# A dense layer with SiLU: the first slab of w1 loaded in two halves, on two queues

## The chip, the core and the metric

The kernel runs on one core of a Trainium2 chip. A core has TensorE (matrix products; its weight loads are listed as PEld), VectorE, ScalarE, GpSimd and SyncE, each with its own list of instructions; SyncE and ScalarE also issue the DMA transfers of this kernel. The metric is the device time of one execution in microseconds (us). Lower is better.

## The reference

```python
h = jnp.einsum("bsd,df->bsf", x, w1)     # x 1 x 2048 x 640, w1 640 x 1728, bfloat16
h = jax.nn.silu(h)
out = jnp.einsum("bsf,fd->bsd", h, w2)   # w2 1728 x 640
```

Two matrix products, with SiLU between them; input, weights and result are bfloat16.

## The kernel before

The 2048 rows of x are cut into four chunks of 512. The first product is computed transposed: for a tile of 128 columns of w1 (ft, 13 full tiles and one of 64) and a chunk, the 640 values of the sum are taken in five steps of 128 (k, `DT` = 5). One matmul has a 128 x 128 block of w1 as its weights and a 128 x 512 block of x, transposed, as its moving operand. x arrives transposed by transposing DMAs (`turned`, line 120), one for each chunk and k. w1 goes to `w1s`, w2 to `w2s`, and the last 64 columns and rows are handled apart.

For the first chunk the order is chosen so that work can begin with little data. The first eight tiles (`FA` = 8) are computed k by k (`k_pass`, line 178): pass k takes x's block k and slab k of w1, which is 128 rows of w1 by 1024 columns, 256 KB, and adds into the eight PSUM banks. Before each pass TensorE waits for the transpose `ld_x[k]` and the slab `ld_k[k]` (line 186). After pass 4 the remaining tiles 8 to 12 follow (line 197), from two larger transfers, tiles 8 to 10 and tiles 11 to the end (`FG`, line 117). Then come the other chunks, the 64-column tail, and the second product, whose results are copied out by VectorE and ScalarE and stored by SyncE.

The order of the DMA issues on SyncE is written out by hand: transpose 0, transpose 1, slab 1, transpose 2, slab 2, and so on to slab 4, then the two larger w1 transfers, then the transposes of the other chunks and w2. Slab 0 alone is issued by ScalarE (line 132).

A program begins with a barrier that the framework puts in: each engine drains and reports, GpSimd waits for all reports and lets all go, and each engine waits for that. The kernel moves instructions about it. `ahead_of_start` (line 98) puts an instruction ahead of an engine's drain: the zeroing of `z`, transpose 0 and slab 0. `barrier_wait_here` (line 109) moves an engine's own wait to a later place: for SyncE behind the w1 transfers (line 141), for TensorE behind the dummies (line 167). Dummies (line 161) are matmuls on the zeros in `z`, 256 columns each, whose result nobody reads; twelve of them keep TensorE busy until the first data is there. ScalarE runs one SiLU on a small buffer (line 145), so that its table is loaded early.

Of the kernel before, what the change touches and what calls it, by code (L numbers as in the profile page):

```python
# [9 lines left out]
def bass_standalone__dense_activation_silu__prompt_kernel(  # L10
# [13 lines left out]
    P = 128  # L24
    NB = 8
    BANK = 512
    DT = D // P
# [10 lines left out]
    pe, act, dve, pool, sp = nc.tensor, nc.scalar, nc.vector, nc.gpsimd, nc.sync  # L38

    with ExitStack() as es:  # L40
        def sb(name, shape, dtype):
            return es.enter_context(nc.sbuf_tensor(name, shape, dtype))

        xT = sb("xT", [P, DT, S], bf16)
        w1s = sb("w1s", [P, DT, F], bf16)
# [13 lines left out]
        def sem(name):  # L59
            s = es.enter_context(nc.semaphore(name))  # L60
            count[s.name if hasattr(s, "name") else name] = 0
            return [s, 0]

        def tick(ins, s, n=1):
            ins.then_inc(s[0], n)
            s[1] += n
            return (s, s[1])

        def wait(eng, *points):
            for pt in points:  # L70
                if pt is None:
                    continue
                s, v = pt
                key = (id(eng), id(s))
                if seen.get(key, 0) < v:
                    eng.wait_ge(s[0], v)
                    seen[key] = v
# [6 lines left out]
        def load(eng, out_ap, in_ap):  # L84
            s = sem(f"s_ld{n_dma[0]}")
            n_dma[0] += 1
            return tick(eng.dma_start(out=out_ap, in_=in_ap), s, 16)  # L87

        ET = mybir.EngineType

        def preamble(engine, opcode):
            lst = nc.main_func.blocks[0].instructions
            return next(
                i for i, ins in enumerate(lst)
                if ins.opcode == opcode and ins.engine == engine
            )

        def ahead_of_start(emit, engine):
            lst = nc.main_func.blocks[0].instructions
            n = len(lst)  # L100
            r = emit()
            lst = nc.main_func.blocks[0].instructions
            new = lst[n:]
            del lst[n:]
            at = preamble(engine, "Drain")
            lst[at:at] = new
            return r

        def barrier_wait_here(engine):
            lst = nc.main_func.blocks[0].instructions  # L110
            lst.append(lst.pop(preamble(engine, "EventSemaphore")))

        w1_v = w1.rearrange("(dt p) f -> p dt f", p=P)
        w2_v = w2[0:F0, :].rearrange("(ft p) d -> p ft d", p=P)

        FA = 8
        FG = [(8, 11), (11, FT)]

        def turned(c, dt, s):
            return tick(sp.dma_start_transpose(  # L120
                out=xT[:, dt, c * SCH:(c + 1) * SCH],
                in_=xf[c * SCH:(c + 1) * SCH, dt * P:(dt + 1) * P],
            ), s, 16)

        def load_k(eng, k):
            return load(eng, w1s[:, k, 0:FA * P], w1_v[:, k, 0:FA * P])

        ld_w1 = {}
        s_x = [sem(f"s_x{k}") for k in range(DT)]
        p_z = ahead_of_start(lambda: tick(dve.memset(z[:, :], 0.0), s_dve), ET.DVE)  # L130
        ld_x = [ahead_of_start(lambda: turned(0, 0, s_x[0]), ET.SP)]
        ld_k = [ahead_of_start(lambda: load_k(act, 0), ET.Activation)]
        for k in range(1, DT):
            ld_x.append(turned(0, k, s_x[k]))
            ld_k.append(load_k(sp, k))
        for a, b in FG:
# [24 lines left out]
        def dummies(n):  # L161
            for _ in range(n):
                pe.matmul(ps[:, 3, 0:HB], lhsT=z[:, 0:P], rhs=z[:, :], start=True, stop=True)  # L163

        wait(pe, p_z)
        dummies(12)
        barrier_wait_here(ET.PE)

        def mm(o, l, r, start, stop, shared=False):
            return pe.matmul(o, lhsT=l, rhs=r, start=start, stop=stop, skip_group_check=shared)  # L170

        def silu(out_ap, in_ap, bank, after):
            wait(act, after)
            r = tick(act.activation(out=out_ap, in_=in_ap, func=ACT.Silu), s_act)  # L174
            bank_free[bank] = r
            return r

        def k_pass(k):
            for ft in range(FA):
                ins = mm(ps[:, ft, :], w1s[:, k, ft * P:(ft + 1) * P], xT[:, k, 0:SCH],  # L180
                         start=(k == 0), stop=(k == DT - 1), shared=True)
                if k == DT - 1:
                    silu(hT[:, ft, 0:SCH], ps[:, ft, :], ft, tick(ins, s_pe))

        for k in range(DT):
            wait(pe, ld_x[k], ld_k[k])
            k_pass(k)

        nxt = [FA]

# [169 lines left out]
```

## Time and profile before

| | us |
|---|---|
| median of five executions | 126.42 |
| the five, lowest to highest | 125.83, 125.83, 126.42, 127.14, 127.69 |
| the profiled execution, its own time | 125.92 |
| span of the profiled execution | 124.6 |
| TensorE busy with matmuls | 121.4 (97%) |
| TensorE busy with weight loads | 55.0 (44%) |
| ScalarE busy | 38.2 (31%) |
| VectorE busy | 7.5 (6%) |
| transpose 0, from issue to landing | 3.3 |
| slab 0 (ScalarE), from issue to landing | 2.6 |
| slabs 1 to 4 (SyncE), from issue to landing | 3.1, 3.2, 3.3, 3.4 |

The span runs from the first to the last instruction of one execution; the rest of that execution's time lies around it. All times inside the span count from its start. Line numbers such as L170 are those of the kernel before; L170 is the helper through which all real matmuls go, L163 the dummies, L120 the transposing loads, L87 all other DMA transfers, L345 the framework's own instructions. A name such as SPq is an engine's instruction queue, here SyncE's, and the time beside it is what the issue takes, not the transfer. The landing of a transfer is when its completion is seen.

### The profile page before, as it was taken

The numbers are of one execution on the slowest core, as the hardware profiler recorded it, in microseconds if no ns is written. First come the engines' busy times: TensorE is split into PE (matmuls) and PEld (weight loads), VectorE is DVE, ScalarE is ACT, GpSimd is POOL, SyncE is SP. The second block draws the span as 40 slices with busy tenths as digits, with TensorE's granted clock in tenths as the row PEclk, the third lists the DMA queues.
The fourth block names the chain that finished last, engine by engine and source line by source line (L and its number), as shares of the span: only waits on it lengthen the run. The fifth ranks groups of instructions, "written<-read, shape, count | busy, mean of one in ns | idle before, by whom it ended". The sixth has DMA issues, their size and how long they took to land.

```text
span 124.6 us, 1336 instructions
## 1 busy us (share of the span) xinstructions
PE 121.4 (97%) x575; PEld 55.0 (44%) x586; DVE 7.5 (6%) x12; ACT 38.2 (31%) x66; POOL 0.3 (0%) x5
## 2 busy tenths in 40 slices
PE   8999999999999999999999999999999999999993
PEld 5343444444444444444434444444434444444452
DVE  0000000000000000000002020200012220102021
ACT  3000985555555555555530101010012101010100
POOL 1000000000000000000000000000000000000000
PEclk9999999999999999999999999999999999999999
DMA  5899959444795000000000000000002468111112
GB/s 129 178 231 240 249 114 81 107 104 90 188 388 196 0 5 0 3 0 0 0 0 0 5 0 0 0 0 0 0 0 67 65 216 299 53 53 53 53 59 99
DMA packets 19398, 10.35 MB, mean 83 GB/s; under 512 B 13505, under 2 KB 18753, under 8 KB 19393
## 3 DMA queue, kind: packets, MB, share of 16 engines
q1 hardware_dynamic: 19248, 10.02, 31.6%
q10 hardware_dynamic: 144, 0.26, 0.7%
q8 instruction: 4, 0.07, 0.2%
q14 instruction: 2, 0.01, 0.0%
HBM read 4.51 MB, written 2.62 MB: 57 GB/s over the span
## 4 chain that ended last, share of the span: by engine, by line
PE 87%; SPq 7%; DMA 4%; issue 1%; ACT 0%
PE ps L170 87%; SPq L120 5%; DMA w1s<-in_w_dram 4%; SPq L87 2%; SPq L345 0%; ACT o_sb L232 0%
## 5 line engine op out<-in xcount | busy, mean ns | idle before, releaser
L170 PE MATMUL ps<-xT,w1s 128*128 128x512 bf16 (+1 forms) x275 | 60.0, 385 | 0.5 <-DMA xT<-in_x_dram 0.2
L170 PE MATMUL ps<-w2s,hT 128*128 128x512 bf16 (+2 forms) x216 | 45.2, 366 | 0.3
L170 PEld LDWEIGHTS ps<-xT,w1s 128*128 128x128 bf16 (+1 forms) x280 | 26.5, 100 | 34.1 <-issue 2.8
L174 ACT ACTIVATE hT<-ps 128x512 bf16<-128x512 f32 x52 | 30.1, 606 | 28.6 <-PE ps L170 28.6
L170 PEld LDWEIGHTS ps<-w2s,hT 128*128 128x128 bf16 x221 | 20.9, 98 | 24.4 <-issue 1.1
L232 ACT CAST o_sb<-ps 128x512 bf16<-128x512 f32 (+1 forms) x8 | 4.4, 546 | 42.2 <-PE ps L170 37.2
L230 DVE CAST o_sb<-ps 128x512 bf16<-128x512 f32 (+1 forms) x9 | 6.1, 677 | 101.1 <-PE ps L170 101.1
L170 PE MATMUL ps<-hT,w2s 128*128 128x512 bf16 x51 | 11.3, 379 | 0.1
L170 PEld LDWEIGHTS ps<-hT,w2s 128*128 128x128 bf16 x52 | 5.1, 98 | 6.1
L232 ACT CAST oT<-ps 128x512 bf16<-128x512 f32 x2 | 1.1, 588 | 11.0 <-PE ps L170 11.0
L163 PE MATMUL ps<-z 128*128 128x256 bf16 x12 | 2.7, 419 | 0.4 <-DVE z L130 0.4
L170 PE MATMUL ps<-w2t,hTt 64*128 64x512 bf16 (+2 forms) x17 | 2.2, 366 | 0.0
L230 DVE CAST oT<-ps 128x512 bf16<-128x512 f32 x2 | 1.3, 686 | 13.7 <-PE ps L170 13.7
L163 PEld LDWEIGHTS ps<-z 128*128 128x128 bf16 x12 | 1.6, 144 | 1.0 <-DVE z L130 0.4
L145 ACT ACT_TABLE_LOAD x1 | 1.3, 1283 | 1.9 <-PEq L345 1.9
L174 ACT ACTIVATE hTt<-ps 128x512 bf16<-128x512 f32 x2 | 1.2, 597 | 1.1 <-PE ps L170 1.1
L170 PEld LDWEIGHTS ps<-w2t,hTt 64*128 64x128 bf16 x17 | 0.7, 94 | 1.4 <-issue 0.8
L170 PE MATMUL ps<-hTt,w2t 64*128 64x512 bf16 x4 | 0.6, 381 | 0.0
L170 PEld LDWEIGHTS ps<-hTt,w2t 64*128 64x128 bf16 x4 | 0.1, 94 | 0.4 <-issue 0.4
L145 ACT ACTIVATE warm<-warm 128x32 f32<-128x32 f32 x1 | 0.2, 229 | 0.0
L130 DVE MEMSET z<- 128x128 uint32 x1 | 0.2, 165 | 0.2 <-issue 0.2
L143 POOL MEMSET warm<- 128x32 f32 x1 | 0.1, 124 | 1.5 <-POOLq L345 1.5
(4 smaller groups left out, 0.4 us busy)
## 6 DMA issues: line engine op xcount, KB each, us to landing
out_dram<-o_sb SPq DMA_DIRECT2D x15, 160.0 KB, 1.9
w2s<-in_w_dram SPq DMA_DIRECT2D x1, 1120.0 KB, 5.9
w1s<-in_w_dram SPq DMA_DIRECT2D x4, 256.0 KB, 3.3
w2s<-in_w_dram SPq DMA_DIRECT2D x1, 960.0 KB, 8.1
w1s<-in_w_dram SPq DMA_DIRECT2D x1, 480.0 KB, 4.8
w1s<-in_w_dram SPq DMA_DIRECT2D x1, 400.0 KB, 5.6
xT<-in_x_dram SPq DMA_TRANSPOSE x20, 2.9
w1s<-in_w_dram ACTq DMA_DIRECT2D x1, 256.0 KB, 2.6
```

The lines of the kernel that those rows point to most:

```text
L87: return tick(eng.dma_start(out=out_ap, in_=in_ap), s, 16)
L120: return tick(sp.dma_start_transpose(out=xT[:, dt, c * SCH:(c + 1) * SCH], in_=xf[c * SCH:(c + 1) * SCH, dt * P:(dt + 1) * P],), s, 16)
L130: p_z = ahead_of_start(lambda: tick(dve.memset(z[:, :], 0.0), s_dve), ET.DVE)
L143: p_warm = tick(pool.memset(warm[:, :], 0.0), s_pool)
L145: act.activation(out=warm[:, :], in_=warm[:, :], func=ACT.Silu)
L163: pe.matmul(ps[:, 3, 0:HB], lhsT=z[:, 0:P], rhs=z[:, :], start=True, stop=True)
L170: return pe.matmul(o, lhsT=l, rhs=r, start=start, stop=stop, skip_group_check=shared)
L174: r = tick(act.activation(out=out_ap, in_=in_ap, func=ACT.Silu), s_act)
L230: r = tick(dve.tensor_copy(out=out_ap, in_=in_ap), s_dve)
L232: r = tick(act.copy(out=out_ap, in_=in_ap), s_act)
```

## The change

Slab 0 is cut into two halves of four tiles. ScalarE issues the first half ahead of its drain, SyncE the second half behind transpose 0. Transpose 1 and slab 1 are also put ahead of SyncE's drain. TensorE waits before pass 0 for the first half only, and for the second half between tiles 3 and 4 of pass 0. There are 15 dummies instead of 12, and TensorE's barrier wait moves from behind the dummies to behind pass 0.

```diff
-        ld_k = [ahead_of_start(lambda: load_k(act, 0), ET.Activation)]
-        for k in range(1, DT):
+        FH = FA // 2
+        ld_k0a = ahead_of_start(
+            lambda: load(act, w1s[:, 0, 0:FH * P], w1_v[:, 0, 0:FH * P]), ET.Activation)
+        ld_k = [ahead_of_start(
+            lambda: load(sp, w1s[:, 0, FH * P:FA * P], w1_v[:, 0, FH * P:FA * P]), ET.SP)]
+        ld_x.append(ahead_of_start(lambda: turned(0, 1, s_x[1]), ET.SP))
+        ld_k.append(ahead_of_start(lambda: load_k(sp, 1), ET.SP))
+        for k in range(2, DT):
             ld_x.append(turned(0, k, s_x[k]))
             ld_k.append(load_k(sp, k))
...
         wait(pe, p_z)
-        dummies(12)
-        barrier_wait_here(ET.PE)
+        dummies(15)
...
             for ft in range(FA):
+                if k == 0 and ft == FH:
+                    wait(pe, ld_k[0])
...
         for k in range(DT):
-            wait(pe, ld_x[k], ld_k[k])
+            wait(pe, ld_x[k], ld_k[k] if k else ld_k0a)
             k_pass(k)
+            if k == 0:
+                barrier_wait_here(ET.PE)
```

## Prediction, made before the changed kernel was run

> **What bounds the kernel now.** I read the chain of waits first, because the page gives TensorE 97% busy and a change at the start can only pay if something at the start holds the end.
>
> ```profile
> 1.25 0.05 issue
> 1.30 0.37 SPq L345
> 1.67 0.07 issue
> 1.74 1.14 SPq L120
> 2.88 0.05 issue
> 2.94 0.57 SPq L87
> 3.51 0.06 issue
> 3.57 1.12 SPq L120
> ...
> 8.27 0.04 issue
> 8.31 0.58 SPq L87
> 8.89 0.04 issue
> 8.93 4.79 DMA w1s<-in_w_dram
> 13.72 0.05 issue
> 13.77 10.32 PE ps L170 x47
> ```
>
> Columns: start, length, what. Up to 8.93 us the end hangs on SyncE writing out DMA issues one after another, then on one transfer (w1 columns of tiles 8 to 10), which lands at 13.72. From there it is TensorE without a hole to the end. So each us added to SyncE's list before 8.93 is added to the end, if the transfer keeps its 4.79 us; TensorE work before 13.7 counts only if it becomes later than that landing.
>
> How much later could it be? The timeline of the start shows TensorE's rate:
>
> ```profile
> 0.39 2.74 PE L163 MATMUL ps<-z 128*128 128x256 bf16 x12 [0.39 <-DVE z L130]
> ...
> 3.34 0.13 PEld L170 LDWEIGHTS ps<-xT,w1s 128*128 128x128 bf16 x2 [0.69 <-DMA xT<-in_x_dram]
> ...
> 3.75 0.15 PEld L170 LDWEIGHTS ps<-xT,w1s 128*128 128x128 bf16 x1 [0.28 <-issue]
> 4.17 0.15 PEld L170 LDWEIGHTS ps<-xT,w1s 128*128 128x128 bf16 x1 [0.27 <-issue]
> ```
>
> Weight loads, one per tile, start 0.427 us apart up to 6.31 us. The windows of the later passes hold eight tiles in 1.72 to 1.73 us (6.53 to 8.25, 8.25 to 9.98), 0.216 each. So the whole pass k=0, eight tiles, ran at half rate (3.34 to about 6.5), and full rate began near 6.31, although the granted clock reads 1.00 in every window. Pass 3 then began at 10.00 instead of 9.98 and pass 4 at 11.81 instead of 11.72, both on w1; the tiles after pass 4 could have begun at 13.54 but waited to 13.77. Without these three waits (0.02 + 0.09 + 0.23) TensorE would have been there at 13.43: its cover is 0.34 us.
>
> **The change part by part.** The sum is made against the profiled execution: span 124.6 us, its own time 125.92, so 1.32 lies around the span. The median of the runs shown is 126.42, 0.50 above it.
>
> *Half of slab 0 from ScalarE to SyncE.* ScalarE's one issue (0.38 us at 0.12) stays one issue. SyncE gets one more, between transposes 0 and 1. All four w1 issues that follow a transpose take 0.57 to 0.58 us, the two that follow another load 0.43 and 0.53; the new one follows a transpose, and ScalarE's whole slab also has one row per partition, so half the bytes need not shorten it: 0.575 + 0.05 for the step between = 0.625 us on SyncE.
>
> *Transpose 1 and slab 1 ahead of SyncE's drain.* They were behind it; the order of the DMAs among themselves stays, only the drain moves.
>
> ```profile
> L345 ACTq DRAIN  x1: 145/145/145, 0.5 to 0.5; - x1
> L345 SPq DRAIN  x1: 367/367/367, 1.3 to 1.3; - x1
> ```
>
> SyncE's drain behind a transpose took 0.367, ScalarE's behind a plain load 0.145. The new place is behind a plain load. New list of SyncE: transpose 0 to 1.25; half slab 1.30 to 1.87; transpose 1 from 1.92 (was 1.74); slab 1 from 3.10 (was 2.94); drain from 3.72; transpose 2 from 3.94 with the short drain, 4.16 with the long one (was 3.57). Everything behind, tiles 8 to 10 too, is late by 0.37 to 0.59. I take 0.37, since what stands before an issue visibly matters (0.58 against 0.43 above).
>
> Does that reach the landing? Two readings. The Trainium skill, page "DMA: Bandwidth & Descriptors", section "Issuing engines are not separate DMA queues", says that all issuers share the same 16 DMA engines and that spreading issues saves only the sequencer's time, "which is usually small relative to the DMA itself". By that the same bytes arrive at the same time and the sum is 0: 125.92. The row says otherwise: slabs 1 to 4, issued every 1.79 us, land 3.1, 3.2, 3.3 and 3.4 us after issue, nearly constant, so there the issue sets the pace and the DMA engines follow. Only the 0.3 us of growth, and 4.79 for the last transfer, show some backlog, which could swallow a part of the delay. By the row the sum is +0.37. Bounds: 0 (all swallowed) and +0.59.
>
> *The first transpose beside half the traffic.* It landed 3.30 us after issue, the second 2.8, with fewer bytes beside it: at best 0.5 us earlier. Worth nothing here, because of the next part.
>
> *Three more dummies.* Twelve started 0.213 us apart from 0.39; fifteen occupy TensorE to about 3.57. The first real matmul moves from 3.34 to 3.57: +0.23, on TensorE alone. The work until full rate is then 0.23/0.427 = 0.53 tile less, made up at 0.216 each: +0.115 us later at tile 8, 13.55 against the 13.43 above. Cover: the landing at 13.72 + 0.37 = 14.09. Cost nothing; without that cover, 0.12.
>
> When does full rate begin? The page "TensorE: Matmul & The Clock Gate", Part 1, gives half clock by default and full clock after a busy window of about 3.4 us that runs freely, not from the kernel's start. By the row, 6.31, the forecast stands. By the rule with dummies counted from 0.39 it may begin anywhere from 3.8 to 7.2. At 3.8 TensorE gains (6.31 - 3.8)/2 = 1.25 us and loses it all in waits for w1; at 7.2 it loses 0.45, still inside the new cover of 14.09 - 13.55 = 0.54. The trace has one phase only.
>
> *A wait in the middle of pass 0* for the second half of slab 0. Behind it on TensorE are tiles 4 to 7 and all later work. It is needed at 3.57 + 4 x 0.427 = 5.27. Issued at 1.30, it lands between 3.9 (ScalarE's slab, 2.6 us) and 4.7 (the slowest slab, 3.4). I take 4.4, by slab 1's 3.1. Cost nothing; the cover is 0.6 to 1.4 us. Transpose 1 and slab 1 shift by 0.16 to 0.18, so slab 1 lands at 6.2, needed at 6.6.
>
> *Barrier.* SyncE's drain now ends at 3.9 to 4.1 instead of 1.67, so the other engines are let go 2.2 to 2.4 us later: ScalarE's table load from 1.89 to about 4.2, done with its warm-up by 5.8; its first real activation is at 12.2. VectorE and GpSimd have nothing due. TensorE's own wait now stands behind pass 0, which ends after 5.3 at any clock: free. Cover 6 us and more than 1 us.
>
> Sum: +0.37 on the landing, the rest hidden: 125.92 + 0.37 = 126.29 for an execution like the profiled one, 126.42 + 0.37 = 126.8 for a median like the one shown.
>
> **Rivals.** *Swallowed:* the DMA backlog takes the delay in, and the landing stays near 13.72. For it: growing landing times, 4.79 for the last one. Against it: the even pace before. TensorE's 13.55 is still covered: 125.9 by the profile, 126.4 by the median.
>
> *Fewer late starts of the full clock:* the five runs spread by 1.86 us, more than a DMA floor explains; if in some of them TensorE reached full rate late because of the idle 0.2 us between dummies and transpose, the unbroken dummies would bring all to the floor. The floor itself is up by 0.37, so 126.3 in the median; to be over 1% faster (under 125.16) it would have to beat the shortest run, 125.83, by 0.7, for which I find no mechanism.
>
> *Slower: full rate comes one window later.* If zeros, or the later start of real work, put it off by 3.41 us to 9.7, then 14.4 tiles run at 0.427 and 25.6 at 0.216 from 3.57 on: tile 8 at 15.24, against 13.77: +1.47, 127.4 by the profile and 127.9 by the median. It decides from about 7.4 us on, where TensorE passes the landing at 14.09. For it: the spread of the runs before, which such phases would give. Against it: 12 dummies with a hole sufficed at 6.31, and 15 without a hole give no less activity.
>
> *It does not do what it says:* splitting the slab was to start pass 0 sooner; with dummies to 3.57 it starts later whatever lands. That is inside the forecast.
>
> **How the numbers follow.** The landing moves by 0.2 to 0.6: chance 0.50, 126.8. Swallowed 0.17, 126.4. Fewer late starts 0.11, 126.3. A later full clock 0.22, 127.9. The range leaves out the tails: 125.9 (swallowed, with a median half a us low, as the spread allows) to 127.9. A change under 1%, 1.26 us, is what a measurement of this kernel can hardly tell from none, with runs from 125.83 to 127.69. Of the first three cases 0.06 may fall below 125.16 for reasons I do not see; the later clock gives 0.21 over 127.68.
>
> **What would show it.** In the changed kernel's profile: transpose 2 issued at 3.9 to 4.2; the tiles 8 to 10 transfer issued at 9.3 to 9.5 and landing at 14.1 to 14.3, again the last wait before an unbroken TensorE; first real matmul at 3.57; no wait in pass 0. The forecast is wrong if w1 lands no later than 13.8, if the spacing stays 0.427 beyond 7.4 us, or if TensorE halts in the middle of pass 0.

## The result and the profile after

| | kernel before | changed kernel |
|---|---|---|
| median of all executions | 126.49 us (79) | 126.28 us (44) |
| lowest to highest | 125.28 to 127.69 | 125.72 to 127.14 |
| lowest tenth below, highest tenth above | 125.54, 127.46 | 125.81, 126.60 |
| profiled execution, its span | 125.92, 124.6 | 126.19, 124.9 |

The ratio is 1.0004, 95% interval 0.9988 to 1.0019: no change. This ratio leaves out executions more than 1.5% above the fastest of the same kernel, which here takes 14 of 79 from the kernel before and none from the changed one; the medians and tenths above count all. They show what one number hides: the lowest tenth rose by 0.27 us, the highest fell by 0.86.

The chain of waits of the changed kernel, start, length, what (from here on, line numbers are those of the run that is shown; in the changed kernel L169 is the dummies, L175 the helper of the real matmuls, L354 the framework):

```profile
1.25 0.06 issue
1.31 0.56 SPq L87
1.87 0.06 issue
1.93 1.14 SPq L120
3.07 0.04 issue
3.12 0.58 SPq L87
3.69 0.06 issue
3.75 0.13 SPq L354
3.88 0.07 issue
3.94 1.13 SPq L120
...
8.70 3.50 DMA w1s<-in_w_dram
12.19 0.14 issue
12.33 0.59 PE ps L175 x2
```

SyncE's list stands as forecast: the new half-slab issue at 1.31, the drain (L354) at 0.13, transpose 2 at 3.94 for 3.57. But the last wait is now slab 4, issued at 8.70, landing at 12.19 (11.68 before). The transfer of tiles 8 to 10, the last wait before, landed at 13.64 (13.72 before) although it was issued 0.39 later: it took 4.3 us for 4.8. Slab 4 held pass 4 until 12.33, and tile 8 began eight tiles later, at 14.05, against 13.77: +0.28.

The timeline of the start:

```profile
0.39 3.38 PE L169 MATMUL ps<-z 128*128 128x256 bf16 x15 [0.39 <-DVE z L130]
...
3.57 5.61 PE L175 MATMUL ps<-xT,w1s 128*128 128x512 bf16 x20
...
4.42 0.15 PEld L175 LDWEIGHTS ps<-xT,w1s 128*128 128x128 bf16 x1 [0.28 <-issue]
4.85 0.78 PEld L175 LDWEIGHTS ps<-xT,w1s 128*128 128x128 bf16 x4 [0.28 <-issue]
```

Real work begins at 3.57 with no idle time given in brackets: transpose 0 landed 2.9 us after issue (3.3 before) and had to wait for the dummies. Full rate began near 4.9 to 5.1 us, in the middle of pass 0.

So there are two questions: what makes the highest times of the kernel before, and what takes them away? Is the risen lowest tenth the price of the issue on SyncE?

### The profile page after: what moved, and what is told of

Its sections match the earlier page's. It is cut to its first block, busy times and chain, and to the rows that moved or that the text cites. A ratio compares the mean times of both kernels' runs of the same rounds, so it can differ in the third digit from the quotient of the medians.

```text
span 124.9 us, 1343 instructions
## 1 busy us (share of the span) xinstructions
PE 121.3 (97%) x578; PEld 55.4 (44%) x589; DVE 7.5 (6%) x12; ACT 38.1 (31%) x66; POOL 0.3 (0%) x5
## 4 chain that ended last, share of the span: by engine, by line
PE 88%; SPq 7%; DMA 3%; issue 1%; ACT 0%
PE ps L175 88%; SPq L120 5%; DMA w1s<-in_w_dram 3%; SPq L87 2%; ACT o_sb L241 0%; SPq L354 0%
## 5 line engine op out<-in xcount | busy, mean ns | idle before, releaser
L175 PE MATMUL ps<-xT,w1s 128*128 128x512 bf16 (+1 forms) x275 | 59.6, 382 | 0.8 <-DMA w1s<-in_w_dram 0.3
L175 PE MATMUL ps<-w2s,hT 128*128 128x512 bf16 (+2 forms) x216 | 45.0, 366 | 0.4 <-issue 0.2
L175 PEld LDWEIGHTS ps<-xT,w1s 128*128 128x128 bf16 (+1 forms) x280 | 26.4, 99 | 33.8 <-issue 3.2
L175 PEld LDWEIGHTS ps<-w2s,hT 128*128 128x128 bf16 x221 | 20.9, 98 | 24.4 <-issue 1.1
L175 PE MATMUL ps<-hT,w2s 128*128 128x512 bf16 x51 | 11.3, 379 | 0.1
L175 PEld LDWEIGHTS ps<-hT,w2s 128*128 128x128 bf16 x52 | 5.1, 98 | 6.1
L169 PE MATMUL ps<-z 128*128 128x256 bf16 x15 | 3.4, 419 | 0.4 <-DVE z L130 0.4
L169 PEld LDWEIGHTS ps<-z 128*128 128x128 bf16 x15 | 2.1, 145 | 1.2 <-DVE z L130 0.4
L175 PE MATMUL ps<-w2t,hTt 64*128 64x512 bf16 (+2 forms) x17 | 2.2, 366 | 0.0
L175 PEld LDWEIGHTS ps<-w2t,hTt 64*128 64x128 bf16 x17 | 0.7, 94 | 1.4 <-issue 0.8
L175 PE MATMUL ps<-hTt,w2t 64*128 64x512 bf16 x4 | 0.6, 382 | 0.0
L175 PEld LDWEIGHTS ps<-hTt,w2t 64*128 64x128 bf16 x4 | 0.1, 94 | 0.4 <-issue 0.4
```

## Experiments

Three groups ran, each on one chip with its own executions of the kernel before. The medians of the kernel before on these chips were 127.09, 126.95 and 126.60, so times are compared inside a group only. Each "ratio" is to the kernel before on the same chip. "Hole" is the idle time of TensorE between the end of the last dummy and the first real tile; a dummy's end is its start plus 0.213. Landings, holes and the onset of full rate are those of the one execution of each kernel that was profiled, while a median stands for 13 to 22 executions (66 to 73 of the kernel before).

### First group: dummies, hole, split

15 dummies alone.

```diff
-        dummies(12)
+        dummies(15)
```

> The kernel before with 15 dummies for 12 and nothing else. Theory (two effects that cancel: the extra SyncE issue raises the fastest executions by 0.4 us, the unbroken dummies take away executions in which TensorE reaches full rate late): no extra issue here, so the fastest stay near 125.3 and only the spread goes: median 125.7 to 125.9, highest below 126.8, ratio 0.995. Rival (the dummies do nothing, the spread goes with the way in which the loads are issued): median 126.4 to 126.6, highest 127.5 or more, as before.

Measured: median 126.34 against 127.09, ratio 0.9944 (0.9918 to 0.9971). Shorter, but not narrow as expected: the tenths are 125.82 and 127.42, against 126.38 and 127.62 for the kernel before. Transpose 0 landed at 3.87 here, so a hole of 0.35 was left even behind 15 dummies; real work began at 3.92, at full rate from its first tile.

The changed kernel with 12 dummies.

```diff
-        dummies(15)
+        dummies(12)
```

> The changed kernel with 12 dummies for 15. Theory: fastest at 125.7 by the extra issue, and the wide spread comes back: median 126.7 to 126.9, highest 127.6 or more, ratio 1.003. Rival (the spread goes with the loads): as the changed kernel, median 126.2 to 126.3, highest below 127.1.

Measured: median 126.42, ratio 0.9960 (0.9937 to 0.9983), highest 127.23. A miss for the theory: with 12 dummies the median stays 0.67 below the kernel before. The timeline tells why:

```profile
0.39 2.74 PE L169 MATMUL ps<-z 128*128 128x256 bf16 x12 [0.39 <-DVE z L130]
3.00 0.13 PEld L175 LDWEIGHTS ps<-xT,w1s 128*128 128x128 bf16 x2 [0.35 <-DMA xT<-in_x_dram]
```

With the slab split, transpose 0 landed at 2.96 and real work began at 3.01, when 12 dummies had just ended (2.93). It is not the number of dummies; it may be the hole.

15 dummies, the hole kept: three of them stand behind the wait for the first data.

```diff
         dummies(12)
         barrier_wait_here(ET.PE)
+        wait(pe, ld_x[0], ld_k[0])
+        dummies(3)
```

> The kernel before, with three further dummies behind the wait for transpose 0 and slab 0: 15 in number, but the hole of 0.4 us before real work stays, and real work starts 0.64 us later, near 3.98. Theory with the hole as the cause: spread as wide as before, and the late executions later by up to 0.3: median 126.5 to 126.8, highest 127.7 or more. Rival (the number of dummies or the time they run is the cause): narrow, as with 15 in one piece: median 125.8 to 126.1, highest below 127.

Measured: median 127.26 against 127.09 for the kernel before, ratio 1.0003 (0.9976 to 1.0030), and 126.34 for 15 in one piece; highest 128.04. So the gain of 15 dummies is gone, as the theory had it. Its timeline:

```profile
0.39 2.74 PE L163 MATMUL ps<-z 128*128 128x256 bf16 x12 [0.39 <-DVE z L130]
4.02 0.35 PEld L163 LDWEIGHTS ps<-z 128*128 128x128 bf16 x3 [1.36 <-DMA xT<-in_x_dram]
...
4.64 6.58 PE L172 MATMUL ps<-xT,w1s 128*128 128x512 bf16 x19
...
8.90 0.15 PEld L172 LDWEIGHTS ps<-xT,w1s 128*128 128x128 bf16 x1 [0.27 <-issue]
9.33 1.61 PEld L172 LDWEIGHTS ps<-xT,w1s 128*128 128x128 bf16 x8 [0.28 <-issue]
```

Transpose 0 landed at 3.97, the hole was 1.1 us, and weight loads stayed 0.427 us apart up to 9.33. Tile 8 began at 15.59, two us after its data (13.50). This profiled execution took 127.71, one of the longest of its kernel. No wait for a transfer explains that, only the spacing does.

The changed kernel without the split: slab 0 whole on ScalarE, transpose 1 and slab 1 still ahead of the drain.

```diff
-        FH = FA // 2
-        ld_k0a = ahead_of_start(
-            lambda: load(act, w1s[:, 0, 0:FH * P], w1_v[:, 0, 0:FH * P]), ET.Activation)
-        ld_k = [ahead_of_start(
-            lambda: load(sp, w1s[:, 0, FH * P:FA * P], w1_v[:, 0, FH * P:FA * P]), ET.SP)]
+        ld_k = [ahead_of_start(lambda: load_k(act, 0), ET.Activation)]
         ld_x.append(ahead_of_start(lambda: turned(0, 1, s_x[1]), ET.SP))
         ld_k.append(ahead_of_start(lambda: load_k(sp, 1), ET.SP))
...
```

The rest of the edit takes out the wait in the middle of pass 0.

> The changed kernel without the split: slab 0 whole on ScalarE, transpose 1 and slab 1 ahead of SyncE's drain, 15 dummies, TensorE's barrier wait behind pass 0. SyncE has no further issue, and its drain stands behind a plain load (0.13 us for 0.37): transpose 2 is issued at 3.3 for 3.57 before and 3.94 in the changed kernel. Theory: all landings behind are 0.25 us earlier than before; fastest 125.1, narrow spread, median 125.5 to 125.7, ratio 0.993. Rival (the landings are set by the DMA engines, not by the issue): fastest and median as with 15 dummies alone, 125.3 and 125.8, no gain from the drain. Rival (dummies do nothing): median 126.2 or more.

Measured: median 126.05, ratio 0.9943 (0.9907 to 0.9978); transpose 2 issued at 3.43. The median, of 13 executions, is 0.29 below 15 dummies alone, but the ratios are alike (0.9943, 0.9944), so a gain from the moved drain is not shown. The highest tenth is 127.18: transpose 0 landed at 4.40, which leaves a hole of 1.1 even behind 15 dummies. In the profiled execution that did no harm: the last three dummies start 0.17 and 0.11 us apart instead of 0.213, so full rate had come near 3.05, within the dummies, and it outlasted the hole.

### Second group: where the second half goes

> The changed kernel once more, beside the next three on the same chip. Theory, reformed after the first four runs (the split matters because transpose 0 lands at 2.9 instead of 3.3 to 4.4 us, so no hole stands between dummies and real work; the half slab on SyncE costs 0.4 us in the fastest executions): narrow, 90% of executions within 0.9 us, against 1.2 us or more for the kernel before; median 0.2 to 0.6 below the kernel before.

Measured: the same changed kernel, median 126.40 against 126.95, ratio 1.0007 (0.9971 to 1.0043). Nine of 14 executions lie within 126.17 to 126.52, but five between 127.23 and 127.99, so the narrow spread did not come. The profiled execution, at 126.17, is none of the five; it had no hole, and full rate from about 6.05. Whether the five had a hole was not recorded.

The changed kernel without the split, with 12 dummies (the diff is to the same kernel with 15):

```diff
         ld_x.append(ahead_of_start(lambda: turned(0, 1, s_x[1]), ET.SP))
         ld_k.append(ahead_of_start(lambda: load_k(sp, 1), ET.SP))
...
-        dummies(15)
+        dummies(12)
```

> The changed kernel without the split and with 12 dummies: transpose 1 and slab 1 ahead of SyncE's drain, slab 0 whole on ScalarE. Theory: transpose 0 lands at 3.3 to 4.4, the hole behind 12 dummies is 0.4 us or more, so the executions spread as in the kernel before; the earlier issues gain at most 0.25 us and only in the fastest: median 0 to 0.2 below the kernel before, highest as there. Rival (the moved drain, not the split, makes the executions narrow): median as the changed kernel with 12 dummies, 0.5 below the kernel before, and highest 0.7 below it.

Measured: median 126.89 against 126.95, ratio 0.9994 (0.9969 to 1.0018), highest 127.66. Without the split, the moved drain gives nothing behind 12 dummies. Transpose 0 landed at 4.32, the hole was 1.4 us, and full rate began near 8.6, in an execution of 127.20:

```profile
4.37 6.97 PE L171 MATMUL ps<-xT,w1s 128*128 128x512 bf16 x22 [1.24 <-DMA xT<-in_x_dram]
...
8.19 0.15 PEld L171 LDWEIGHTS ps<-xT,w1s 128*128 128x128 bf16 x1 [0.28 <-issue]
8.59 2.47 PEld L171 LDWEIGHTS ps<-xT,w1s 128*128 128x128 bf16 x12 [0.25 <-issue]
```

Both halves on ScalarE, the second behind the barrier; SyncE's list and TensorE's barrier wait are those of the kernel before:

```diff
...
+        ld_k[0] = load(act, w1s[:, 0, FH * P:FA * P], w1_v[:, 0, FH * P:FA * P])
         wait(act, p_warm)
...
```

> Both halves on ScalarE: the first ahead of its drain as in the changed kernel, the second behind the barrier at 1.8 us, when transpose 0 is on its way; SyncE's list is that of the kernel before, with its drain between transposes 0 and 1; 15 dummies. Theory: transpose 0 lands near 2.9, real work from 3.57 without a hole, second half lands near 4.3 to 4.6 (needed at 5.3, or at 4.5 with an early full clock); transpose 2 issued at 3.57 instead of 3.94, so landings 0.3 to 0.4 us before those of the changed kernel: median 0.3 to 0.4 below it, as narrow. Rival (the DMA engines set the landings): median equal to the changed kernel's within 0.1.

Measured: median 127.26, 0.31 above the kernel before (ratio 1.0018, 0.9993 to 1.0043, not clear of noise) and 0.86 above the changed kernel. Both theories missed. Its chain:

```profile
3.57 1.12 SPq L120
...
8.93 6.12 DMA w1s<-in_w_dram
15.05 0.05 issue
15.10 9.67 PE ps L174 x44
```

Issue times are those of the kernel before, but the transfer of tiles 8 to 10 took 6.1 us for 4.8. Transpose 1, with the second half beside it on the other queue, landed at 5.2, against 4.5 to 4.7 in the four profiles with the same list and the whole slab ahead of the drain, and all behind it landed 0.5 to 1.3 later than in the kernel before. In this trace the second queue saved SyncE's issue time and cost more in the transfers. It also shows a late end with no hole and with full rate from about 4.2: 127.25, by the transfers alone.

The same with transpose 1 and slab 1 ahead of the drain, TensorE's barrier wait behind pass 0, and the second half freed from the barrier:

```diff
...
-        p_warm = tick(pool.memset(warm[:, :], 0.0), s_pool)
-        ld_k[0] = load(act, w1s[:, 0, FH * P:FA * P], w1_v[:, 0, FH * P:FA * P])
+        p_warm = ahead_of_start(lambda: tick(pool.memset(warm[:, :], 0.0), s_pool), ET.Pool)
         wait(act, p_warm)
         act.activation(out=warm[:, :], in_=warm[:, :], func=ACT.Silu)
+        ld_k[0] = load(act, w1s[:, 0, FH * P:FA * P], w1_v[:, 0, FH * P:FA * P])
+        barrier_wait_here(ET.Activation)
...
```

> As the kernel with both halves on ScalarE, and transpose 1 and slab 1 ahead of SyncE's drain; so that the later barrier does not hold the second half, GpSimd's zeroing of the warm-up buffer goes ahead of its drain and ScalarE's barrier wait behind its warm-up and the second half (issued near 2.3 us). Theory: transpose 2 issued near 3.4, 0.5 before the changed kernel; median 0.4 to 0.6 below the changed kernel, narrow. Rival: transpose 1, issued at 1.3, or the second half competes with transpose 0 again; it lands past 3.6, the hole is back, and the spread with it.

Measured: median 126.30, ratio 0.9956 (0.9930 to 0.9982), 0.10 below the changed kernel, highest tenth 127.38. The rival was right: the second half went out at 0.84 already (the table load had begun at 0.78 and did not hold it up), transpose 0 landed at 4.36 and left a hole of 0.8. In the profiled execution the hole did no harm; real work ran at full rate from its first tile at 4.40.

### Third group: the hole once more, and a better version

> The changed kernel a third time, as the measure for the next three on the same chip. Expected: transpose 0 lands near 2.9, real work from 3.57 without a hole, full rate by 7.2 us; median 126.2 to 126.4.

Measured: 126.29 (125.97 to 126.69) against 126.60 for the kernel before, ratio 0.9967 (0.9944 to 0.9990). As expected, transpose 0 landed at 2.86 and left no hole.

The split kept, the hole brought back by taking dummies away:

```diff
-        dummies(15)
+        dummies(8)
```

> The changed kernel with 8 dummies for 15: they end at 2.1, transpose 0 still lands near 2.9, so a hole of 0.8 us stands before real work although the slab is split. Theory (the split helps because it closes the hole): [...]full rate begins between 5.5 and 8.9 us; the executions spread again, median 0.2 to 0.5 above the changed kernel with 15. Rival (the split helps by the landings alone): as the changed kernel within 0.1, or faster, since real work starts 0.6 us earlier.

Measured: median 126.34, highest 127.19. The median is 0.05 above the changed kernel, within the rival's 0.1, and the theory's 0.2 to 0.5 did not come. The ratio, though, is 1.0018 (0.9995 to 1.0042), above the 0.9967 with 15 dummies, so a small loss is not excluded. In the profile a hole of 0.78 us did no harm:

```profile
0.39 1.89 PE L169 MATMUL ps<-z 128*128 128x256 bf16 x8 [0.39 <-DVE z L130]
2.85 0.13 PEld L175 LDWEIGHTS ps<-xT,w1s 128*128 128x128 bf16 x2 [1.05 <-DMA xT<-in_x_dram]
...
4.11 0.15 PEld L175 LDWEIGHTS ps<-xT,w1s 128*128 128x128 bf16 x1 [0.27 <-DMA w1s<-in_w_dram]
4.44 0.53 PEld L175 LDWEIGHTS ps<-xT,w1s 128*128 128x128 bf16 x3 [0.18 <-issue]
```

Full rate came by 4.44, before the 5.5 of the theory. So a hole as such is not enough: 0.78 was harmless even behind 8 dummies, 1.1 and 1.4 behind 12 went with full rate at 9.3 and 8.6. Nor does the length alone decide: with the drain moved and 15 dummies 1.1 was harmless, since full rate had come before it.

18 dummies in the kernel before, which reach to 4.2 us:

```diff
-        dummies(12)
+        dummies(18)
```

> The kernel before with 18 dummies: they run to 4.2 us and cover transpose 0 even where it lands beside the whole slab at 3.9 to 4.2. Theory: no hole, no late full rate, no extra issue on SyncE: median 0.3 to 0.5 below the changed kernel, 0.6 or more below the kernel before, and as narrow as the changed kernel. Rival (real work that starts at 4.2 is late itself): median at or above the changed kernel.

Measured: median 125.92, ratio 0.9952 (0.9927 to 0.9977), 0.37 below the changed kernel. Transpose 0 landed at 3.86, real work began at 4.21 without a hole:

```profile
0.39 4.02 PE L163 MATMUL ps<-z 128*128 128x256 bf16 x18 [0.39 <-DVE z L130]
...
4.21 7.14 PE L170 MATMUL ps<-xT,w1s 128*128 128x512 bf16 x31
...
4.63 1.18 PEld L170 LDWEIGHTS ps<-xT,w1s 128*128 128x128 bf16 x6 [0.27 <-issue]
```

The start of real work at 4.21, against 3.34 in the profile of the kernel before, cost nothing. The loads are those of the kernel before, yet the tenths are 125.67 and 126.32 against 125.71 and 127.49: most of the spread of the kernel before comes with its 12 dummies, not with its loads.

The changed kernel without the split and with 18 dummies (the diff is to the same kernel with 15):

```diff
-        dummies(15)
+        dummies(18)
```

> The changed kernel without the split and with 18 dummies: whole slab on ScalarE, transpose 1 and slab 1 ahead of SyncE's drain. With 15 dummies a hole of up to 1.0 us was left. Theory: hole at most 0.3, median 0.0 to 0.2 below the kernel before with 18 dummies, and below the changed kernel by 0.3 to 0.6. Rival (transpose 1 beside transpose 0 and the slab backs up the DMA engines): slab 4 lands as late as in the changed kernel, at 12 us or later, and the median equals that of the changed kernel within 0.1.

Measured: median 125.71 (125.09 to 126.38), ratio 0.9936 (0.9911 to 0.9961): 0.89 below the kernel before and 0.58 below the changed kernel on the same chip. Against 18 dummies alone it is 0.21 lower, but the intervals of the ratios overlap. Its chain:

```profile
3.24 0.12 SPq L348
3.35 0.07 issue
3.42 1.12 SPq L120
...
8.16 3.62 DMA w1s<-in_w_dram
11.79 0.14 issue
11.92 110.61 PE ps L171 x541
```

Slab 4 lands at 11.79, 0.52 before the changed kernel on this chip (12.31), as much earlier as transpose 2 is issued (3.42 for 3.94), and the rival's landing at 12 or later did not come. In this pair the landing follows the issue, and that is the price of the half slab on SyncE. That the figures agree so closely is luck, since single traces scatter: with the changed kernel's list slab 4 landed between 11.99 and 12.53 in five profiles, with that of the kernel before between 11.68 and 12.17 in four, and with the shorter list of this kernel between 11.79 and 12.86 in three.

## Why the prediction was right

The forecast, no change at 126.8 in a range of 125.9 to 127.9, held, but the measured median, 126.28, lies 0.5 below its 126.8 and did not come about as the sum had it. Two effects cancel, and only one was in the sum; that they are of one size is luck.

*SyncE's list: right.* Transpose 2 was issued at 3.94 with the short drain (0.13), as taken.

*The landing: the right sign, another transfer.* The forecast had tiles 8 to 10 land at 14.1 to 14.3 as the last wait. They landed at 13.64, and w1 landing no later than 13.8 was one of the prediction's own signs of being wrong. Their transfer took the delay in, which the rival "swallowed" had foreseen. But slab 4, which held pass 4 by only 0.09 us before, landed 0.52 later and became the last wait. Tile 8 moved by 0.28, not 0.37, and the lowest tenth by 0.27.

*Dummies, middle wait, barrier: right.* Real work began at 3.57; the second half, landed at 3.90, was waited for by nobody; ScalarE's table load began at 4.10, well ahead of a first activation at 12.74. Two readings were off without harm. Of the eight tiles of pass 0 seven, not all, ran at half rate before. And 3.8 was not the earliest full rate: in two profiles it came near 3.05 and 3.25. As said of an early full rate, its gain went into waits for w1: pass 0 was done early, and pass 1 waited for slab 1 until 6.26.

*"The first transpose beside half the traffic", "worth nothing here": wrong, and this is the step that failed.* The profiled execution of before had transpose 0 at 3.30 and looked covered; the idle 0.2 us that the prediction names is the hole of 0.42 here, counted from the modelled end of the last dummy. In the other three profiles with the SyncE list of the kernel before and the whole slab 0 on ScalarE, transpose 0 landed at 3.87, 3.97 and 3.86; where ScalarE's queue had only half of the slab before 1.9 us, at 2.80 to 2.96. Behind 12 dummies, which end at 2.93, that makes holes of 0.4 to 1.1 us, and in the profiles with 1.1 and 1.4 behind 12 dummies full rate came late. I had worked out this mechanism (half rate one window longer, +1.5 us) as the slower rival, and placed it in the changed kernel; the experiments point to the kernel before. The rival "fewer late starts of the full clock", given 0.11 and called limited by the higher floor, is what they support, together with the higher floor.

*The sum on the median* therefore added 0.37 to a median that held late executions: in the third group three quarters of its executions took 125.97 us or more, longer than the median of the same kernel with 18 dummies, 125.92. The floor of an execution and the median of a kernel need separate sums where executions spread by 2%.

How far is the hole shown as the cause? Against each other stand 15 dummies in one piece and 15 with the hole kept (126.34, 127.26), and 18 dummies against 12 in the kernel before (125.92, 126.60), with the same loads in each pair. (The kernel with the hole kept also starts real work later, at 4.64; a start at 4.21 cost nothing in the second pair.) No late execution of the kernel before was itself profiled, so that it looks like the late ones shown above is argued, not shown. Argued too is why one hole delays full rate and another does not. The Trainium skill, page "TensorE: Matmul & The Clock Gate", Part 1, has a free-running window of about 3.4 us that must be busy, without saying how busy. Laid on the traces, counted back from the onset of full rate, it fits: the window that ended with full rate held the hole of 0.42 us in the kernel before (6.31) and 0.78 with 8 dummies; the one that ended at 2.90 in the kernel before, idle for 0.90 of its 3.41, brought none, and neither did those that held the holes of 1.1 and 1.4 us, ending near 5.9 and 5.2. No run measured the share by itself. That half rate is that page's half clock is not shown either: the granted clock of every profile read 1.00, and only the spacing, 0.427 against 0.216 us, tells the two rates apart. Why 5 of 14 executions of the changed kernel ended late on one chip stays open; the kernel with both halves on ScalarE shows that late transfers can do it without a hole.

## What to carry to other kernels

Where the first real work waits for a DMA, let the dummies reach past the latest landing that several profiles show, not the one in a single profile: surplus dummies are free as long as a later landing sets the pace, as here with 18. Before an issue is moved onto the queue whose list is the chain of waits, price it there (0.58 us and the step between), and look for the same effect without one: here six more dummies alone gave 0.7 us (126.60 to 125.92). When a change leaves the median alone, compare the tenths.

## What was not expected of the hardware

A plain load on ScalarE's queue went with a later landing of the transposing load beside it on SyncE's queue, by amounts that differ. Transpose 0 took 2.8 to 3.0 us from issue to landing beside 128 KB on ScalarE's queue. Beside 256 KB it took 3.3 to 4.0 with transpose 1 issued near 1.75, and 4.0 to 4.4 with transpose 1 issued at 1.3 already. A half slab issued at 1.90 beside transpose 1 went with a landing of that transpose at 5.2 instead of 4.5 to 4.7, and with a whole series of transfers late, the last one by 1.3 us. SyncE's drain took 0.12 to 0.13 us behind a plain load and 0.37 to 0.38 behind a transpose. The granted clock read 1.00 in the profiles also where tiles ran 0.427 us apart.
